# Three pairs of hidden blocks by seven half products in the last batch's first FFN product, and another order of the sums behind it

## The chip, the core and the metric

The kernel runs on one core of a Trainium2 chip. The time is the device time of one execution in microseconds (us), and the median of several executions is compared. A core has these engines: TensorE (PE, matrix products from SBUF into PSUM; loading the stationary operand is listed apart as PEld), VectorE (DVE), ScalarE (ACT), GpSimd (POOL) and SyncE (SP, which here issues output DMAs). Each works through its own instructions in the order in which the program wrote them, and waits on semaphores for the others. PSUM, where products accumulate, has eight banks of 512 fp32 columns.

## The reference

Attention with a band of local keys and 32 global tokens, then a feed-forward network (FFN) on all tokens. Here the second part matters:

```
x = attn_out.transpose(0, 2, 1, 3).reshape(8 * 544, 512)    # 8 batches, 32 global + 512 local rows each
h = x @ w_in                                                # 512 -> 2048
g = h * (1.0 / (1.0 + np.exp(-1.702 * h)))                  # "gelu" below
out = (g @ w_out).astype(np.float32)                        # 2048 -> 512
```

## The kernel before

The program is written in one fixed order, without a scheduler: an engine meets its instructions in the order in which the code names them. The local rows of batch `i` are one tile of 512 tokens, `xL[i]`, with features on the partitions. The first FFN product makes the 2048 hidden features as 16 **blocks** of 128 features by 512 tokens; the gelu of block `fc` goes to `gTs[i][:, fc]`. Two neighbouring blocks, `2g` and `2g+1`, are **pair** `g`.

A **direct step**, `h_step(i, fc)` (L663), takes a PSUM bank, runs four matmuls of 512 columns (`h_mm`, L636) and has ACT write the gelu (`h_act`, L659). Four banks (`pbank`) go round among these steps and other uses.

A pair can also be made with seven **half products** in place of the eight that two blocks of two token halves need (a Strassen-like scheme; a half product is two matmuls of 256 columns). That is class `HPair` (L698), for one pair or two at once: its PSUM tiles are `x` and `y` (of two banks each, from `spair`; one bank of each is used for a single pair), its sums of weights (`wh`) and of inputs (`xs`) are ready beforehand. Below, one use of it is called a triple of stages, or short a **triple**, whose operations are:

- `mm(3, 4)`: products 3 and 4 into the two halves of `x`; `m3`: ACT copies the half with 3 to an SBUF tile `zz`; `z` (L728): DVE adds the half with 4 to it;
- `mm(1, 6)`: products 1 and 6 into the two halves of `y`; `zm` (L731): DVE adds the half with 1 to `zz` as its other half;
- `mm(5, 2)`: accumulated on both halves of `x`; `sub` (L734): DVE takes `x` from `zz`; `inner`: ACT writes the gelu of `x`, which is two of the pair's four quarters;
- `mm(7)`: accumulated on the first half of `y`; `add` (L737): DVE adds `y` to `zz`; `outer`: ACT writes the gelu of `zz`, the other two quarters.

The second FFN product uses seven products as well, in class `Pair` (L796, matmuls in L821). Its operands are halves of `gTs[i]` and four arrays of sums and differences, which DVE makes in `g_sums(i, lo, hi, which)` (L785; L791 for array 2, L794 for arrays 0, 1 and 3) for the pairs `lo` to `hi - 1`, once their gelus are there. Product 3 reads the even blocks' first half of the tokens directly from `gTs`, product 4 the odd blocks' second half; 1, 6, 5 and 7 read arrays 0, 1, 2 and 3 (5 and 2 both read array 2).

`h_some(i)` (L1207) is the first FFN product of the batches 3 to 7. For 3 to 6 it has work of the next batches between (names `c` and `a2`), makes the pairs 1 and 2 in one triple and the rest directly, and returns early. For the last batch, 7, `c` and `a2` are `None`: it makes pair 1 in one triple, pair 4 in a second and the other twelve blocks directly. The sums of the gelus stand between its steps.

Behind it comes the tail (L1324 to L1378): the 256 global rows' first product (batch "B", 16 direct steps of four matmuls of 256 columns, `xG`) with the last batch's second product between its steps (`todo`, L1330), then the global rows' second product and the last stores. The tail's banks for `Pair` (`psX`) are the ones that `HPair` used. SP's queue holds the output stores; POOL only has two of the last ones here.

Of the kernel before, what the change touches and what calls it, by code (L numbers as in the profile page):

```python
# [20 lines left out]
def kernel(  # L21
# [53 lines left out]
    def load(b, us=(0, 1), kq=True):  # L75
        if b not in loaded:
            loaded[b] = (ld.tile([128, 2, 16 * D], BF16, name="rk"),
                         ld.tile([128, 2, 16 * D], BF16, name="rq"))
        if kq:
            s = slice(us[0], us[-1] + 1)  # L80
            nc.gpsimd.dma_start(out=loaded[b][1][:, s], in_=qf[b][:, s])
            nc.gpsimd.dma_start(out=loaded[b][0][:, s], in_=kf[b][:, s])
# [157 lines left out]
    def transpose_g(lo, hi, names="qk"):  # L240
        for name, dst, s in (("q", qgT, rqg), ("k", kgT, rkg)):
            if name not in names:
                continue
            nc.vector.transpose(dst[:, lo:hi, :32], s[:, lo:hi].bitcast(F32))
# [35 lines left out]
    def pbank(name):  # L280
        return psP.tile([128, 512], F32, name=name, tag="p")
# [349 lines left out]
    def width(i):  # L631
        return TB if i < B else B * Sg
# [3 lines left out]
    def h_mm(i, fc, hp, kcs):  # L636
        for kc in kcs:
            nc.tensor.matmul(hp[:, : width(i)], lhsT=w_in_c[:, fc // 4, kc, fc % 4 // 2, :, fc % 2],  # L638
                             rhs=(xL[i] if i < B else xG)[:, kc, :],
                             start=(kc == 0), stop=(kc == NKC - 1))  # L640
# [18 lines left out]
    def h_act(i, fc, hp):  # L659
        n = width(i)  # L660
        gelu(gTs[i][:, fc, :n], hp[:, :n])

    def h_step(i, fc):  # L663
        if fc == 0:
            gTs[i] = (moe.tile([128, FC, TB], BF16, name="gT") if i < B else
                      early.bitcast(BF16).rearrange("p a b -> p (a b)").rearrange("p (f t) -> p f t", f=FC))
        hp = pbank("hp")
        h_mm(i, fc, hp, range(NKC))
        h_act(i, fc, hp)
# [100 lines left out]
    def parts_of(i):  # L770
        n = width(i)
        t = gTs[i].rearrange("p (g e) t -> p g e t", e=2)
        return [t[:, :, e, h * n // 2 : h * n // 2 + n // 2] for h in range(2) for e in range(2)]

    def g_sums(i, lo, hi, which=(0, 1, 2, 3)):
        n = width(i)
        if i not in sums:
            if i < B:
                sums[i] = [moe.tile([128, FC // 2, w * HT], BF16, name="gs%d" % k)
                           for k, w in enumerate((1, 1, 2, 1))]  # L780
            else:
                room = [ld.tile([128, 2, 16 * D], BF16, name=x).rearrange("p a b -> p (a b)")
                        for x in ("rk", "rq", "rk")]
                sums[i] = [x.rearrange("p (g t) -> p g t", g=FC // 2)
                           for x in (room[0][:, :1024], room[0][:, 1024:], room[1], room[2][:, :1024])]  # L785
        a11, a12, a21, a22 = parts_of(i)
        t = gTs[i].rearrange("p (g e) t -> p g e t", e=2)
        g = slice(lo, hi)
        for k in which:
            if k == 2:  # L790
                nc.vector.tensor_tensor(sums[i][2][:, g, :n], t[:, g, 0, :n], t[:, g, 1, :n], ALU.add)  # L791
            else:
                x, y, op = {0: (a11, a22, ALU.add), 1: (a21, a11, ALU.subtract), 3: (a12, a22, ALU.subtract)}[k]
                nc.vector.tensor_tensor(sums[i][k][:, g, : n // 2], x[:, g], y[:, g], op)  # L794
# [75 lines left out]
    a, c = Quad(0), Quad(1)  # L870
# [94 lines left out]
    a, c = nq[1]  # L965
# [71 lines left out]
    a, c = nq[2]  # L1037
# [30 lines left out]
    def quads_of(n):  # L1068
        if n < B and n not in nq:
            nq[n] = (Wide(2 * n), Wide(2 * n + 1))  # L1070
        return nq.get(n, (None, None))
# [135 lines left out]
    def h_some(i):  # L1207
        c = nq[i + 1][1] if i + 1 < B else None
        a2 = quads_of(i + 2)[0] if i + 2 < B else None
        pool = nc.gpsimd.tensor_copy  # L1210
        gTs[i] = moe.tile([128, FC, TB], BF16, name="gT")
        hps = [pbank("hp"), pbank("hp")]
        for fc in range(2):
            h_mm(i, fc, hps[fc], range(NKC))
        gs = (1, 2) if c else (1,)
        fcs = iter([fc for fc in range(2, 8) if fc // 2 not in gs])
        p = HPair(i, *gs)
        p.mm(3, 4)
        p.m3()
        for fc in range(2):  # L1220
            h_act(i, fc, hps[fc])
        if c:
            if i + 3 < B:
                load(i + 3)
            c.kcopy(pool)
            c.qcopy(pool)
            c.ext((3,), pool)
        if a2:
            a2.Tk(False)
        p.z()  # L1230
        p.mm(1, 6)
        p.zm()
        if a2:
            a2.Tq(False)
            transpose_g(2 * i + 4, 2 * i + 6)
        h_step(i, next(fcs))
        if c:
            c.ext((0,), on_act)
        h_step(i, next(fcs))
        p.mm(5, 2)  # L1240
        p.sub()
        p.inner()
        p.mm(7)
        p.add()
        if not c:
            h_step(i, next(fcs))
            p.outer()
            h_step(i, next(fcs))
        else:
            g_sums(i, 0, 1)  # L1250
            h_step(i, 8)
            p.outer()
            g_sums(i, 1, 4)
            h_step(i, 9)
            c.ext((1,), on_act)
            h_step(i, 10)
            c.ext((2,), on_act)
            h_step(i, 11)
            h_step(i, 12)
            h_step(i, 13)  # L1260
            g_sums(i, 4, 7, (0, 1, 3))
            h_step(i, 14)
            h_step(i, 15)
            return
        p = HPair(i, 4)
        p.mm(3, 4)
        p.m3()
        g_sums(i, 0, 2, (0, 1))
        p.z()
        p.mm(1, 6)  # L1270
        p.zm()
        g_sums(i, 0, 2, (2,))
        h_step(i, 10)
        h_step(i, 11)
        p.mm(5, 2)
        p.sub()
        p.inner()
        p.mm(7)
        p.add()
        g_sums(i, 0, 2, (3,))  # L1280
        h_step(i, 12)
        p.outer()
        for k in range(3):
            for lo in (2, 4):
                g_sums(i, lo, lo + 2, (k,))
        h_step(i, 13)
        h_step(i, 14)
        h_step(i, 15)
        g_sums(i, 6, 8, (0, 1, 2))
        g_sums(i, 2, 4, (3,))  # L1290
        g_sums(i, 4, 6, (3,))
        g_sums(i, 6, 8, (3,))

    for i in range(1, B):
        if i > 2:
            h_some(i)
        elif i > 1:
            for fc in range(FC):
                h_step(i, fc)
                if i == 2 and fc == 0:  # L1300
                    weight_sums(1, 2)
                if i + 1 < B:
                    c = nq[i + 1][1]
                    if fc == 1:
                        c.Tk()
                        c.Tq()
                        c.ext((3,))
                    if fc in (3, 5, 7):
                        c.ext(((3, 5, 7).index(fc),), on_act)
                    if fc == 9 and i + 2 < B:  # L1310
                        a2 = quads_of(i + 2)[0]
                        a2.T()
                        transpose_g(2 * i + 4, 2 * i + 6)
                        a2.ext()
                if fc in (4, 8, 12):
                    g_sums(i, fc // 2 - 2, fc // 2)
                if fc == 13:
                    g_sums(i, 6, 7)
        if i == 1:
            phase_o1()  # L1320
        elif i + 1 < B:
            phase_o(i)
# [4 lines left out]
    def pair_banks(k):  # L1327
        return [psX.tile([128, 512], F32, name="x", tag="x%d" % (2 * (k % 2) + j)) for j in range(2)]

    todo = [(tt, k) for tt in range(2) for k in (3, 4, 1, 6, 5, 2, 7)]  # L1330
    for st in range(FC):
        h_step(B, st)
        if st < len(todo):
            tt, k = todo[st]
            if k == 3:
                p = Pair(B - 1, tt, pair_banks(tt))
# [19 lines left out]
    p = Pair(B, 0, (x0, x1, y0, y1))  # L1356
# [53 lines left out]
```

## Time and profile before

| | |
|---|---|
| median of three runs | 284.22 us (284.15, 284.22, 285.25) |
| the profiled execution | 284.39 us |
| its span, from first to last instruction | 282.7 us |
| last batch's first product on PE (starts in the timeline) | 240.21 to 253.62 us |
| busy from 240.20 to 254.06 us: PE, DVE, ACT, POOL | 13.86, 9.47, 10.79, 0.00 us |

A line of the page or of an answer names the line of the code, the engine, the operation, and the program's tiles as output<-input with their shapes; "xN" is the number of instructions in a group. In a line of the timeline, the first number is the start in us from the span's start, the second the time from there to the end of the group; in brackets stands the idle time ahead of it and what ended it. The chain of work that ended last goes back from the last instruction to what released it, step by step. The starts of matmuls are good marks; their ends are modelled, so that groups overlap a little in the list. An elementwise instruction on DVE or ACT can start a little (some 0.1 us) before the one ahead of it on its engine is listed as ended, where it doesn't need its result. The names in the lines: `s` is the tile of `HPair`'s `x` and `y`, `ob` the one of its `zz`, `hp` a direct step's bank, `gs` the arrays of sums, `px`, `py` and, in the tail, `x` the banks of the second product.

### The profile page before, as it was taken

To read this page: it belongs to the slowest core of one execution; us is meant where nothing else is said; L and a number is where in the kernel's file an instruction comes from. 1 tells how busy PE (TensorE), PEld (TensorE's weight loads), DVE (VectorE), ACT (ScalarE), POOL (GpSimd) and SP (SyncE) were. 2 spreads that over 40 slices of the span, in tenths; PEclk is the share of its full clock that TensorE was granted. 3 is DMA by queue.
4 is the path that set the end of the run, shared out by engine and by line. 5 is a ranking of instruction groups with operands and counts; after the bars stand their busy time and mean duration, and the time that the engine had idled before them with its cause. 6 is when DMAs were issued, how large, how long until landed. Compare 5 with 4: busy or idle time off the path is not lost.

```text
span 282.7 us, 9018 instructions
## 1 busy us (share of the span) xinstructions
PE 277.0 (98%) x3787; PEld 185.5 (66%) x3787; DVE 227.6 (81%) x486; ACT 186.9 (66%) x319; POOL 112.3 (40%) x161
## 2 busy tenths in 40 slices
PE   8999999999999999999999999999999999999994
PEld 7554445544554488756886488757876589558884
DVE  7687368996689898989998899899997898586452
ACT  4847657577778785489756994689648961873331
POOL 8984550856936004970099206940080000000001
PEclk9999999999999999999999999999999999999999
DMA  7999996999999804994089807930023003300223
GB/s 207 155 191 205 204 174 84 146 218 157 165 172 175 151 2 58 93 156 90 12 108 131 148 5 91 86 70 2 20 62 74 2 2 77 74 2 1 58 54 113
DMA packets 59352, 28.24 MB, mean 100 GB/s; under 512 B 47472, under 2 KB 49776, under 8 KB 59312
## 3 DMA queue, kind: packets, MB, share of 16 engines
q0 software_dynamic: 51760, 17.83, 57.1%
q1 hardware_dynamic: 7120, 9.18, 11.8%
q8 instruction: 29, 0.48, 0.7%
q10 hardware_dynamic: 432, 0.66, 0.7%
q14 instruction: 11, 0.09, 0.1%
HBM read 36.31 MB, written 8.91 MB: 160 GB/s over the span
## 4 chain that ended last, share of the span: by engine, by line
PE 93%; DMA 2%; DVE 2%; ACT 1%; SPq 0%; issue 0%; DVEq 0%
PE hp L638 32%; PE px L821 13%; PE op L752 10%; PE py L821 9%; PE x L821 6%; PE s L560 6%; PE s L720 5%; PE ov L586 5%; PE s L638 3%; DMA early<-in_q_l_dram 2%; DVE xL L471 1%; PE og L597 1%; PE s L357 1%; ACT e L388 1%; PE s L340 1%; PE ov L438 1%
## 5 line engine op out<-in xcount | busy, mean ns | idle before, releaser
L638 PE MATMUL hp<-xL,w_in_sb 128*128 128x512 bf16 x400 | 90.1, 379 | 0.2 <-DVE xL L471 0.2
L638 PEld LDWEIGHTS <-w_in_sb 128*128 128x128 bf16 x496 | 48.2, 98 | 48.1 <-issue 0.4
L643 ACT ACTIVATE gT<-hp 128x512 bf16<-128x512 f32 x100 | 57.1, 602 | 13.4 <-PE hp L638 13.0
L571 ACT ACTIVATE e<-s 128x1016 bf16<-128x1016 f32 (+1 forms) x56 | 53.3, 1003 | 17.9 <-PE s L560 17.9
L98 POOL DMA_DIRECT2D v<-in_v_l_dram x40 | 31.0, 779 | 61.3 <-PE og L597 52.6
L821 PEld LDWEIGHTS <-gs 128*128 128x128 bf16 x480 | 46.3, 98 | 6.4
L794 DVE TENSOR_TENSOR gs<-gT 128x256 bf16<-128x256 bf16 (+2 forms) x75 | 28.2, 406 | 4.7 <-ACT gT L643 4.7
L576 POOL TENSOR_TENSOR e<-e,mask 128x1760 bf16<-128x1760 bf16 (+1 forms) x7 | 23.1, 3305 | 19.1 <-ACT e L571 19.0
L821 PE MATMUL py<-wsum,gs 128*128 128x256 bf16 x240 | 30.3, 273 | 0.0
L752 PE MATMUL op<-w_out_sb,gT 128*128 128x512 bf16 x128 | 29.5, 380 | 0.0
L854 POOL DMA_DIRECT2D out_dram<-ob x2 | 1.2, 597 | 65.1 <-ACT ob L113 64.9
L576 DVE TENSOR_TENSOR e<-e,mask 128x1712 bf16<-128x1712 bf16 (+1 forms) x21 | 22.1, 1053 | 3.3 <-ACT e L571 3.1
L512 DVE STREAM_TRANSPOSE kT<-rk 128x512 f32<-128x512 f32 x14 | 14.7, 1047 | 11.0 <-DMA rk<-in_k_l_dram 11.0
L752 PEld LDWEIGHTS <-gT 128*128 128x128 bf16 x128 | 11.8, 98 | 14.0
L821 PEld LDWEIGHTS <-gT 128*128 128x128 bf16 x192 | 18.0, 98 | 2.9
L821 PE MATMUL px<-w_out_sb,gT 128*128 128x256 bf16 x160 | 19.2, 273 | 0.0
L821 PE MATMUL px<-w_out_sb,gs 128*128 128x256 bf16 x160 | 19.1, 273 | 0.0
L471 DVE TENSOR_TENSOR xL<-ov,rs 128x512 bf16<-128x512 f32 x27 | 17.9, 686 | 0.7 <-PE ov L438 0.3
L113 ACT ACTIVATE ob<-px 128x512 f32<-128x512 f32 x10 | 6.0, 599 | 18.7 <-DVE zz L843 18.7
L560 PEld LDWEIGHTS <-kT 32*128 32x128 bf16 x672 | 12.5, 93 | 6.8 <-issue 5.3
L643 ACT ACTIVATE gT<-s 128x1024 bf16<-128x1024 f32 (+1 forms) x10 | 9.3, 938 | 11.1 <-DVE ob L734 6.6
L791 DVE TENSOR_TENSOR gs<-gT 128x1024 bf16<-128x1024 bf16 (+3 forms) x21 | 15.9, 761 | 0.0
(182 smaller groups left out, 458.8 us busy)
## 6 DMA issues: line engine op xcount, KB each, us to landing
out_dram<-ob SPq DMA_DIRECT2D x128, 64.0 KB, 2.5
rq<-in_q_l_dram POOLq DMA_DIRECT2D x5, 512.0 KB, 5.2
rk<-in_k_l_dram POOLq DMA_DIRECT2D x5, 512.0 KB, 7.9
v<-in_v_l_dram POOLq DMA_DIRECT2D x24, 96.0 KB, 4.0
w_in_sb<-in_moe_w_in_dram POOLq DMA_DIRECT2D x8, 256.0 KB, 7.8
w_out_sb<-in_moe_w_out_dram POOLq DMA_DIRECT2D x4, 512.0 KB, 10.1
rk<-in_k_l_dram POOLq DMA_DIRECT2D x5, 256.0 KB, 7.4
rq<-in_q_l_dram POOLq DMA_DIRECT2D x5, 256.0 KB, 6.9
```

What stands on the lines that cost most here:

```text
L98: nc.gpsimd.dma_start(out=vt[0:n, hs, c, :D], in_=vs[FIRST[c] : FIRST[c] + n, hs])
L471: nc.vector.tensor_mul(self.x[:, 2 * self.u + h, :], self.st[1 + h], self.st["rs"])
L512: nc.vector.transpose(flat[:, 0:Sl].rearrange("p (r t) -> p t r", t=16), loaded[self.b][0][:, self.u].bitcast(F32))
L560: nc.tensor.matmul(bank(self.ps, j)[:, at : at + n], lhsT=self.k[p, KEYS[c] : KEYS[c] + 128, e], rhs=qs[p, :, :, e], start=(e == 0), stop= ...
L571: nc.scalar.activation(self.E[rnd][:, 2 * i : 2 * i + 2, :n], self.ps[i][:, :, :n], AF.Exp, scale=scale)
L576: eng.tensor_mul(e, e, mask[:, rnd : rnd + 1, :n].to_broadcast([128, 4, n]))
L638: nc.tensor.matmul(hp[:, : width(i)], lhsT=w_in_c[:, fc // 4, kc, fc % 4 // 2, :, fc % 2], rhs=(xL[i] if i < B else xG)[:, kc, :], start=( ...
L643: nc.scalar.activation(out_, in_, AF.Gelu_apprx_sigmoid)
L752: nc.tensor.matmul(op, lhsT=gTs[i][:, fc, tci * 128 : tci * 128 + 128], rhs=w_out_sb[:, fc, :], start=(first and fc == 4 * f4), stop=(fc = ...
L791: nc.vector.tensor_tensor(sums[i][2][:, g, :n], t[:, g, 0, :n], t[:, g, 1, :n], ALU.add)
L794: nc.vector.tensor_tensor(sums[i][k][:, g, : n // 2], x[:, g], y[:, g], op)
L821: nc.tensor.matmul(out_, lhsT=lv[:, g, tt * 128 : tt * 128 + 128], rhs=rv[:, g, :], start=(g == 0 and k in ((1, 3, 4, 6) if self.apart els ...
```

## The change

Only `h_some` is changed, and only for the last batch. The first triple makes the pairs 1 and 2 at once, as in the batches before. The direct steps are then 0, 1, 6, 7 and 10 to 15. The sums of pair 0 are made between the first triple's `zm` and `sub`. Steps 11 and 12 come before the second triple (pair 4), and only step 13 between its `mm(1, 6)` and its `mm(5, 2)`, where two steps were. The sums of the pairs 1 to 3 stand in two parts: arrays 0 and 1 between the second triple's `zm` and `sub`, arrays 2 and 3 behind its `add`. The sums of the pairs 4 to 7 come last, in the order of the arrays.

```diff
-        gs = (1, 2) if c else (1,)
+        gs = (1, 2)
         fcs = iter([fc for fc in range(2, 8) if fc // 2 not in gs])
...
         p.mm(1, 6)
         p.zm()
+        if not c:
+            g_sums(i, 0, 1)
...
         p.inner()
         p.mm(7)
         p.add()
-        if not c:
-            h_step(i, next(fcs))
-            p.outer()
-            h_step(i, next(fcs))
-        else:
+        if c:
             g_sums(i, 0, 1)
             h_step(i, 8)
             p.outer()
...
             return
+        h_step(i, 10)
+        p.outer()
+        h_step(i, 11)
+        h_step(i, 12)
         p = HPair(i, 4)
         p.mm(3, 4)
         p.m3()
-        g_sums(i, 0, 2, (0, 1))
         p.z()
         p.mm(1, 6)
         p.zm()
-        g_sums(i, 0, 2, (2,))
-        h_step(i, 10)
-        h_step(i, 11)
+        g_sums(i, 1, 4, (0, 1))
+        h_step(i, 13)
         p.mm(5, 2)
         p.sub()
         p.inner()
         p.mm(7)
         p.add()
-        g_sums(i, 0, 2, (3,))
-        h_step(i, 12)
+        g_sums(i, 1, 4, (2, 3))
+        h_step(i, 14)
         p.outer()
-        for k in range(3):
-            for lo in (2, 4):
-                g_sums(i, lo, lo + 2, (k,))
-        h_step(i, 13)
-        h_step(i, 14)
         h_step(i, 15)
-        g_sums(i, 6, 8, (0, 1, 2))
-        g_sums(i, 2, 4, (3,))
-        g_sums(i, 4, 6, (3,))
-        g_sums(i, 6, 8, (3,))
+        for k in range(4):
+            g_sums(i, 4, 8, (k,))
```

## The prediction

> **What bounds the kernel now.** I read the page's first two parts first (who is busy, at which clock), then the chain of work that ended last, in order of time, from the last batch on.
>
> ```profile
> PE 277.0 (98%) x3787; PEld 185.5 (66%) x3787; DVE 227.6 (81%) x486; ACT 186.9 (66%) x319; POOL 112.3 (40%) x161
> PEclk9999999999999999999999999999999999999999
> PE 93%; DMA 2%; DVE 2%; ACT 1%; SPq 0%; issue 0%; DVEq 0%
> ```
>
> TensorE (PE) is the bound: 93% of the chain is its own work, at the full granted clock. The chain in order of time, around the change:
>
> ```profile
> 240.37 1.73 PE hp L638 x8
> 242.10 0.87 PE s L720 x8
> ...
> 249.68 0.66 PE s L720 x6
> 250.33 3.89 PE hp L638 x20
> 254.22 0.87 PE x L821 x8
> ...
> 273.00 6.13 PE x L821 x56
> 279.15 0.42 DVE ob L1378
> ```
>
> From 240.37 to 279.13 us each piece begins where the last one ended. So in the last batch PE never waits, whatever PE saves there comes off the end, and whatever PE is made to wait there is added to it. Times below are starts in the timeline (some 0.16 us before the chain's), where the stage begins at 240.21 and the last batch's direct blocks end at 253.62.
>
> **PE work removed and added.** Before, one pair of blocks (2 and 3) and one more (8 and 9) are made with seven half products, the other twelve blocks directly; after, blocks 4 and 5 too go by half products. The chain gives eight full matmuls (one direct pair) 1.73 us, so 216 ns each, and eight half matmuls 0.87 us, so 109 ns each. A direct pair is 8 x 216 = 1.73 us; seven products of two matmuls are 14 x 109 = 1.53 us. PE does **0.20 us less**. Nothing else leaves PE, and no DMA, table load or GpSimd instruction is added or moved; the 128 output stores stay where they were on SP's queue.
>
> A rule of the Trainium skill speaks against this term: "TensorE: Matmul & The Clock Gate", section "Back-to-back issue gap", gives about 131 ns per 512-column matmul and 81 ns per 128-column one in a stream of loads and matmuls. On the straight line between them, an estimate from that page, 256 columns take 98 ns, and the pair would cost 14 x 98 - 8 x 131 = 0.32 us more instead of 0.20 less. The rows above (216 and 109 ns) don't agree with it, and they decide.
>
> **The first triple, two pairs at once.** Batch 6 runs the same two-pair triple in the profile, from its stage start at 210.39; adding 29.82 us puts its rows on the last batch. These are the ACT (ScalarE) rows and then the DVE (VectorE) rows there:
>
> ```profile
> 217.91 1.02 ACT L643 ACTIVATE gT<-s 128x1024 bf16<-128x1024 f32 x1 [1.28 <-DVE ob L734]
> 218.83 0.59 ACT L643 ACTIVATE gT<-hp 128x512 bf16<-128x512 f32 x1
> 219.31 1.06 ACT L643 ACTIVATE gT<-ob 128x1024 bf16<-128x1024 f32 x1
> 220.26 0.60 ACT L643 ACTIVATE gT<-hp 128x512 bf16<-128x512 f32 x1
> ```
>
> ```profile
> 216.66 1.22 DVE L734 TENSOR_TENSOR ob<-ob,s 128x1024 f32<-128x1024 f32 x1 [0.67 <-PE s L720]
> 217.98 1.22 DVE L737 TENSOR_TENSOR ob<-ob,s 128x1024 f32<-128x1024 f32 x1
> ```
>
> The reader sees a chain: sub (L734) 0.2 us after its last product, inner gelu only when sub has ended, then one direct gelu, outer gelu 0.11 us after add (L737), then a direct gelu 0.95 us later. On the last batch: sub 246.48, inner 247.73, gelu of block 10 at 248.65, outer 249.13, gelu of block 11 at 250.08. The wider m3 (0.58 us for 0.37) ends at 243.59, z and zm at 0.69 us each end at 245.11, the four sums of pair 0 end at 246.06 (batch 6's take 1.03 us): all before the products that need them (products 5 and 2 arrive at 245.41 and 7 at 246.28), and before sub. They cost **nothing**, hidden under steps 6 and 7; the tightest slack is 0.4 us (sums against sub).
>
> **The second triple, one pair: the first wait.** Unstalled, PE runs steps 10, 11 and 12 from 246.72, products 3, 4, 1, 6 of blocks 8 and 9 from 249.31 (their banks are free: inner ends at 248.75, add at 249.02), step 13 from 250.19, and wants product 5 at **251.05**. But m3 of this triple now stands on ACT behind the gelus of 11 and 12. Gelus follow each other every 0.48 us, so 12 starts at 250.56 and m3 at 251.04. What comes after m3 is in before's own second triple (ACT row, then DVE rows; L728 is z, L731 zm):
>
> ```profile
> 247.86 0.40 ACT L113 ACTIVATE ob<-s 128x256 f32<-128x256 f32 x1
> ```
>
> ```profile
> 248.29 0.42 DVE L728 TENSOR_TENSOR ob<-ob,s 128x256 f32<-128x256 f32 x1
> 248.81 0.42 DVE L731 TENSOR_TENSOR ob<-ob,s 128x256 f32<-128x256 f32 x1
> ```
>
> z 0.43 us after m3's start, zm 0.52 us after z, 0.42 us each. There products 5 and 2 started at 249.51, two steps after product 6, and found all done; after the change one step is left between, and ACT is later. So z runs 251.47 to 251.89 and zm 251.99 to 252.42. Products 5 and 2 overwrite the halves that m3 and z read, and 7 the half that zm reads. From DVE's end to PE's start I take 0.05 us, from the one place where PE waited for DVE (the first xL product of batch 1 ends at 52.81):
>
> ```profile
> 52.12 1.29 DVE L471 TENSOR_TENSOR xL<-s,rs 128x512 bf16<-128x512 f32 x2
> 52.86 0.59 PE L638 MATMUL hp<-xL,w_in_sb 128*128 128x512 bf16 x2 [0.16 <-DVE xL L471]
> ```
>
> Product 5 starts at 251.94 (0.89 us late), 7 at 252.47 for 252.38 (0.09 more): **+0.98 us**. If product 5 could start when m3 alone is done, 7 still waits for zm, with the same sum. Behind product 5 in PE's queue stand steps 14 and 15 and the whole tail; nobody else is held up. Bounds: 0.8 us (all latencies nil) to 1.2 us (0.1 us more at each of two crossings).
>
> **The second wait.** On DVE the sums 0 and 1 of pairs 1 to 3 (1.03 us, as batch 6's two of 768 columns) now stand between zm and sub: sub starts at 253.29, not at 252.6, where its products are there. Then inner at 254.01 (0.60 us), gelu 14 at 254.51, outer at 254.98 (after add, which ends at 254.77) until **255.61**, gelu 15 until 256.09. PE ends step 15 at 254.42 (253.62 - 0.20 + 0.98 = 254.40), does the first step of the last product's global rows to 254.86, and starts product 3 of the output stage (L821): its first four matmuls take 0.44 us, and its fifth loads block 8, whose half the outer gelu writes. It is wanted at 255.30, and can start at 255.72: **+0.42 us**. Bounds: 0 (if sub were taken before the sums) to 0.86 (if the wait stands before the first of the eight). Before, this product's start at 254.06 was ahead of the end of block 15's gelu (253.82 + 0.60 = 254.42), so matmuls wait for the blocks that they read and not for the whole tile; that is why I take 0.42.
>
> **The last sums.** Pairs 4 to 7 are summed after gelu 15: from 256.13, at 0.69 us for 1024 columns three times (L791 shows 684 ns for 1024) and 1.22 for 2048: the four end at 256.8, 257.4, 258.6 and 259.2. Products 1, 6, 5 and 7 want them at 257.9, 259.2, 260.5 and 263. The z of the output stage, queued on DVE behind them, ends at 259.5, and product 5 at 260.5 is the first to need its bank. Slack 1.0 us: **nothing**; beyond that it would cost its excess.
>
> **The sum.** -0.20 + 0.98 + 0.42 = **+1.20 us**. The profiled execution took 284.39 us, 282.7 of them its span; it would be 285.6. The runs shown have a median of 284.22 (284.15 to 285.25), 0.17 below the profiled one, so **285.4 us**, 0.42% more. A difference under 0.5% (1.42 us) is what I count as no change that a measurement of this kernel can tell.
>
> **Rivals.**
> - A. Neither wait: the pairs only save their 0.20 us, **284.0**. For it: PE had no wait at all in this stage before. Against it: the row that puts m3 behind two more gelus. Chance 0.07.
> - B. Only the first wait: sub comes early enough that the outer gelu is done at 255.3, or the wait falls on a later matmul, **285.0**. Against it: the order of DVE's instructions. Chance 0.15.
> - C. Slower: the wait for the outer gelu stands before the first matmul of product 3 instead of the fifth, so that those four (0.44 us) are late too: +1.64, **285.9**, 0.58% more. It decides from 0.22 us on over the sum. For it: waits are set by the program's bookkeeping of parts of a tile, and the outer gelu writes two separate quarters in one instruction. Against it: the 254.06 row. Chance 0.17.
> - D. Half products cost their weight loads: the loads take 98 ns in the rows against 109 ns of spacing, and with full matmuls at a shorter spacing the added pair would lose what it saves and more: with a loss of 0.32 us, +1.72, **285.9**. The page's rule above is this case; the 216 ns rows speak against it. Chance 0.02.
>
> The forecast, both waits as sized, has 0.59 and a range of its own of 285.1 to 285.7. A is within 0.5% as well: no case is faster by more, since PE saves 0.20 us at most. Slower by over 0.5%: C, D and the upper edge of the forecast (0.1 of it, and the spread of the runs), 0.28; faster 0.01; same 0.71. The range reaches from between A and B to beyond C and D with the upper bounds of both waits (1.2 and 0.86 give +1.86): **284.4 to 286.3**.
>
> **What would show it.** Right: the chain no longer runs through PE alone at 251 us but goes over ACT's m3 and DVE's z and zm (L728, L731), with some 0.9 us without matmuls before product 5 of the second triple; the first triple's rows lie at batch 6's times plus 29.82; sub of the second triple starts right behind two sums; a gap of 0.4 us stands inside the first L821 group of eight; and from there to the end everything is shifted alike. Wrong: no gap at 251 (A), an unbroken first L821 group (B) or one that starts late as a whole (C), spacings other than 109 ns in the added triple (D), or a shift that still grows after 256 us, which would mean that the last sums or the output stage's z are late, which I cost at nothing.

## The result, and the profile after

The changed kernel took 286.25 us (median of 7 executions, 285.66 to 286.92) against 284.89 us of the kernel before (7 executions, 284.15 to 285.33) measured beside it: ratio **1.0059, with a 95% interval of 1.0046 to 1.0072** (the medians alone give 1.0048). By the ratio that is slower by a little more than the 0.5% that the prediction took as its bound, where "the same" had the largest chance; the interval reaches below the bound. The profiled execution took 285.66 us, 283.7 of them its span.

The page of the kernel after, engines and chain:

```profile
PE 275.0 (97%) x3770; PEld 185.2 (65%) x3793; DVE 229.0 (81%) x482; ACT 186.8 (66%) x317; POOL 112.3 (40%) x161
PEclk9999999999999999999999999999999999999999
PE 91%; DVE 3%; ACT 3%; DMA 2%; issue 1%; SPq 0%; DVEq 0%; ACTq 0%
```

PE's share of the chain fell from 93 to 91%, ACT's rose from 1 to 3% and DVE's from 2 to 3%. (PE's busy time is no measure here: some matmul records are missing, 23 of them beside 3793 weight loads.) The chain that ended last, in order of time, in the last batch's stage:

```profile
248.30 1.03 PE hp L638 x4
249.33 0.45 PE s L720 x4
...
249.94 1.09 ACT gT L643 x2
251.03 0.28 ACT ob L113
...
251.33 0.43 DVE ob L728
...
251.86 0.42 DVE ob L731
252.28 0.06 DVE gs L794
252.34 0.33 issue
252.66 0.55 DVE gs L794
253.22 0.61 DVE ob L734
...
253.85 1.61 ACT gT L643 x3
255.46 0.05 issue
255.50 0.61 PE x L821 x4
```

Before, PE stood in every line from 240.37 to 279.13. Now the chain leaves PE at 249.8 and comes back at 255.5: two gelus, m3 (L113), z (L728), zm (L731), two sums (L794), sub (L734), then inner, gelu 14 and outer on ACT, and only then the tail's product 3. The same on PE, in the timeline of PE's matmuls after:

```profile
240.06 1.89 PE L638 MATMUL hp<-xL,w_in_sb 128*128 128x512 bf16 x7
...
250.04 1.03 PE L638 MATMUL hp<-xL,w_in_sb 128*128 128x512 bf16 x4
251.81 0.60 PE L720 MATMUL s<-xL,early 128*128 128x256 bf16 x4 [0.74 <-DVE ob L728]
252.33 0.38 PE L720 MATMUL s<-rs,early 128*128 128x256 bf16 x2
252.55 1.89 PE L638 MATMUL hp<-xL,w_in_sb 128*128 128x512 bf16 x8
254.28 0.60 PE L638 MATMUL hp<-xG,w_in_sb 128*128 128x256 bf16 x4
254.71 0.60 PE L821 MATMUL x<-w_out_sb,gT 128*128 128x256 bf16 x4
255.50 0.61 PE L821 MATMUL x<-w_out_sb,gT 128*128 128x256 bf16 x4 [0.19 <-ACT gT L643]
255.95 0.60 PE L638 MATMUL hp<-xG,w_in_sb 128*128 128x256 bf16 x4
```

Before, the same product 3 and the step behind it:

```profile
254.06 1.04 PE L821 MATMUL x<-w_out_sb,gT 128*128 128x256 bf16 x8
254.93 0.60 PE L638 MATMUL hp<-xG,w_in_sb 128*128 128x256 bf16 x4
```

After, the four matmuls of step 13 start at 250.04 and take 0.87 us (four spacings of 216 ns), so product 5 was due at 250.91 and starts at 251.81; the eight matmuls of the tail's product 3 are split after the fourth, which would have been followed at 255.15 and is followed at 255.50.

For all kernels below I read one number, the **stage time**: from the first `hp` group of the last batch to the second `xG` group, both on PE. Before it is 240.21 to 254.93, 14.72 us; after 240.06 to 255.95, 15.89 us: **1.17 us more**, where the prediction has 1.20. After that the tail's pieces run at the same distances in both: 27.75 us to the end of the span.

### The profile page after: what moved, and what is told of

It reads as the page before. It is cut to its first block, busy times and chain, and to the rows that moved or that the text cites. A ratio compares the mean times of both kernels' runs of the same rounds, so it can differ in the third digit from the quotient of the medians.

```text
span 283.7 us, 9001 instructions
## 1 busy us (share of the span) xinstructions
PE 275.0 (97%) x3770; PEld 185.2 (65%) x3793; DVE 229.0 (81%) x482; ACT 186.8 (66%) x317; POOL 112.3 (40%) x161
## 4 chain that ended last, share of the span: by engine, by line
PE 91%; DVE 3%; ACT 3%; DMA 2%; issue 1%; SPq 0%; DVEq 0%; ACTq 0%
PE hp L638 30%; PE px L821 13%; PE op L752 10%; PE py L821 9%; PE x L821 6%; PE s L560 6%; PE s L720 6%; PE ov L586 5%; PE s L638 2%; DMA early<-in_q_l_dram 2%; ACT gT L643 1%; DVE xL L471 1%; PE og L597 1%; PE s L357 1%; ACT e L388 1%
## 5 line engine op out<-in xcount | busy, mean ns | idle before, releaser
L638 PE MATMUL hp<-xL,w_in_sb 128*128 128x512 bf16 x377 | 86.9, 379 | 1.0 <-DVE xL L471 0.2
L638 PEld LDWEIGHTS <-w_in_sb 128*128 128x128 bf16 x488 | 47.4, 98 | 47.1 <-issue 0.4
L643 ACT ACTIVATE gT<-hp 128x512 bf16<-128x512 f32 x98 | 56.1, 603 | 12.7 <-PE hp L638 12.3
L821 PEld LDWEIGHTS <-gs 128*128 128x128 bf16 x480 | 46.2, 98 | 6.5
L794 DVE TENSOR_TENSOR gs<-gT 128x256 bf16<-128x256 bf16 (+3 forms) x72 | 28.0, 417 | 3.7 <-ACT gT L643 3.6
L821 PE MATMUL py<-wsum,gs 128*128 128x256 bf16 x240 | 30.3, 273 | 0.0
L752 PE MATMUL op<-w_out_sb,gT 128*128 128x512 bf16 x122 | 28.8, 380 | 0.5 <-issue 0.3
L821 PEld LDWEIGHTS <-gT 128*128 128x128 bf16 x192 | 17.8, 98 | 3.4 <-ACT gT L643 0.5
L821 PE MATMUL px<-w_out_sb,gT 128*128 128x256 bf16 x160 | 19.2, 273 | 0.0
L821 PE MATMUL px<-w_out_sb,gs 128*128 128x256 bf16 x160 | 19.1, 273 | 0.0
L113 ACT ACTIVATE ob<-px 128x512 f32<-128x512 f32 x10 | 6.0, 599 | 18.7 <-DVE zz L843 18.7
L791 DVE TENSOR_TENSOR gs<-gT 128x512 bf16<-128x512 bf16 (+3 forms) x20 | 15.8, 791 | 0.0
```

The costliest lines, as they stand in the source:

```text
L643: nc.scalar.activation(out_, in_, AF.Gelu_apprx_sigmoid)
L752: nc.tensor.matmul(op, lhsT=gTs[i][:, fc, tci * 128 : tci * 128 + 128], rhs=w_out_sb[:, fc, :], start=(first and fc == 4 * f4), stop=(fc = ...
L821: nc.tensor.matmul(out_, lhsT=lv[:, g, tt * 128 : tt * 128 + 128], rhs=rv[:, g, :], start=(g == 0 and k in ((1, 3, 4, 6) if self.apart els ...
```

## The experiments

The theory: PE waits twice, because m3 stands behind two gelus on ACT whose chain is wider now, and because two sums stand ahead of sub on DVE; nothing else. The rivals are in the expectations. Ratios are against the kernel before on the same chip, beside the same runs.

**The changed kernel again**, without an edit, since 1.17 us is 0.41% and the ratio 0.59%.

> The changed kernel as it is, once more. In its profile the last batch's stage and the start of the tail cost 1.17 us more than before's (the third group of the tail's first steps starts 16.04 instead of 14.87 us behind the stage's start or so, read at the second global step), while the medians are 1.36 us and the ratio of all runs 0.59% (1.7 us) apart. Theory (two waits of PE and nothing else): the profile repeats the two gaps, and the ratio comes out nearer to 1.0041. Rival (something outside this stage costs 0.2 to 0.5 us more): ratio 1.005 to 1.007 again, with a difference of spans or of the time outside the span that the stage does not show.

Measured: ratio 1.0038 (1.0025 to 1.0051), stage time 239.88 to 255.77, 15.89 us. (The two times that the expectation names for the stage are 0.15 us too long; by the marks above they are 14.72 and 15.89.) The stage repeats to the hundredth, the ratio doesn't.

**m3 ahead of the gelus 11 and 12 on ACT.**

```diff
-        h_step(i, 11)
-        h_step(i, 12)
+        hps = [pbank("hp"), pbank("hp")]
+        for fc in (11, 12):
+            h_mm(i, fc, hps[fc - 11], range(NKC))
         p = HPair(i, 4)
         p.mm(3, 4)
         p.m3()
+        for fc in (11, 12):
+            h_act(i, fc, hps[fc - 11])
```

> The changed kernel with the second triple's m3 ahead of the gelus of blocks 11 and 12 on ACT; PE's and DVE's order is kept. Theory (m3's place on ACT sets the first wait): m3 about 1 us earlier, product 5 and 7 of the second triple wait 0.0 to 0.1 us, the second wait stays near 0.4 us (the two sums still stand ahead of sub on DVE); 0.2 to 0.3 us over before, ratio 1.001. Rival (one direct step is too little between products 6 and 5, whatever ACT does, since z and zm take 0.95 us on DVE): the first wait stays at 0.5 us or more, ratio 1.003 or more.

Measured: ratio 1.0008 (0.9994 to 1.0022), stage time 14.91 us, 0.19 over before. m3 starts at 249.89, straight behind outer. PE's rows:

```profile
250.85 0.60 PE L720 MATMUL s<-xL,early 128*128 128x256 bf16 x4
251.52 1.89 PE L638 MATMUL hp<-xL,w_in_sb 128*128 128x512 bf16 x8
...
254.48 0.61 PE L821 MATMUL x<-w_out_sb,gT 128*128 128x256 bf16 x4 [0.20 <-ACT gT L643]
```

The stage began at 240.01, and product 5 starts 10.84 us later, with nothing ahead of it; in the changed kernel it was 11.75. Step 14 follows product 5 by 0.67 us, six matmuls at 109 ns. So the first wait is gone and the second stays: one step between products 6 and 5 is enough once ACT is in time. The rival falls.

**The sums behind add.**

```diff
         p.zm()
-        g_sums(i, 1, 4, (0, 1))
         h_step(i, 13)
...
         p.add()
-        g_sums(i, 1, 4, (2, 3))
+        g_sums(i, 1, 4)
```

> The changed kernel with the arrays 0 and 1 of pairs 1 to 3 summed behind the second triple's add, with arrays 2 and 3, and not between zm and sub. Theory: the first wait stays (0.9 us ahead of product 5, 0.1 ahead of 7), sub starts about 0.7 us earlier, outer ends before the tail's product 3 wants block 8, so the second wait is gone; the later sums stay within their slack; 0.78 us over before, ratio 1.0027. Rival (the second gap is not made by sub's place, or the sums are what is late next): a gap of 0.3 us or more stays in the first L821 group or moves to product 1, 5 or 2 of the tail, ratio 1.004.

Measured: ratio 1.0032 (1.0018 to 1.0046), stage time 240.35 to 255.87, 15.52 us, 0.80 over before. DVE from zm on, and then the chain behind the first wait:

```profile
252.14 0.42 DVE L731 TENSOR_TENSOR ob<-ob,s 128x256 f32<-128x256 f32 x1
252.73 0.69 DVE L734 TENSOR_TENSOR ob<-ob,s 128x512 f32<-128x512 f32 x1 [0.16 <-PE s L720]
```

```profile
252.09 0.91 PE s L720 x6
253.00 2.16 PE hp L638 x12
255.16 0.87 PE x L821 x8
```

Sub follows zm by 0.59 us (1.27 in the changed kernel, 251.86 to 253.13), and from product 5 on the chain is PE's again; the first L821 group is whole. The first wait is as in the changed kernel. The later sums moved nothing.

**Both edits.**

> Both edits: m3 ahead of the two gelus, and the sums behind add. Theory: no gap on PE from the stage's start to the end; 0.20 us less than before, ratio 0.9993. Rival (something outside the two waits costs time): ratio above 1.001 with an unbroken chain on PE in this stage, the difference then lying elsewhere in the span or outside it.

Measured: ratio 0.9992 (0.9978 to 1.0006), stage time 240.15 to 254.69, 14.54 us, **0.18 less than before**. The chain in this stage is PE alone (but for two pieces of 0.05 us "issue" ahead of these lines):

```profile
248.39 1.03 PE hp L638 x4
249.41 0.87 PE s L720 x8
250.29 0.86 PE hp L638 x4
251.15 0.67 PE s L720 x6
251.82 2.16 PE hp L638 x12
253.98 0.87 PE x L821 x8
```

So the third pair saves what its matmuls save, when nothing waits; a ratio can't tell 0.2 us from nothing.

**The order alone**: the changed kernel's order, with pair 1 alone in the first triple and blocks 4 to 7 as direct steps (6 and 7 stand around `outer`, 10 to 12 behind them).

> The changed kernel's order with the old work: the first triple makes pair 1 alone, blocks 4 to 7 are direct steps; one step between products 6 and 5 of the second triple, and the sums in the new places. Theory (the first wait comes of ACT's backlog behind the two-pair triple, whose sub, inner, add and outer are twice as wide): with one pair ACT keeps up, m3 starts 0.5 us after the gelu of block 12 and about 9.98 us after the stage's start, products 5 and 7 wait 0.0 to 0.1 us; the sums ahead of sub still hold up the outer gelu and product 3 of the tail waits 0.3 us; 0.35 us over before, ratio 1.0012. Rival (the order alone makes the first wait): product 5 waits 0.5 us or more, ratio 1.003 or more.

Measured: ratio 1.0015 (1.0006 to 1.0023), stage time 240.32 to 255.34, 15.02 us, 0.30 over before. Its ACT rows:

```profile
249.82 0.60 ACT L643 ACTIVATE gT<-hp 128x512 bf16<-128x512 f32 x1 [0.27 <-PE hp L638]
250.31 0.38 ACT L113 ACTIVATE ob<-s 128x256 f32<-128x256 f32 x1
```

The gelu of block 12 waits for PE, so ACT has no backlog; m3 comes 0.49 us behind it, 9.99 us after the stage's start (10.83 in the changed kernel, 240.06 to 250.89), and product 5 finds z done. The second wait is there (0.30 us). The first wait needs the two-pair triple and the new order together; the second comes with the order of the sums alone. (The two-pair triple in before's order was not run.)

**Step 14 into the first gap.** `h_step(i, 14)` is moved from behind the sums to behind step 13.

> The changed kernel with step 14 moved ahead of products 5, 2 and 7 of the second triple, so that PE has 0.87 us of work where it waited 0.89 us. Theory (the end is set by the chain m3, z, zm, two sums, sub, inner and add, outer on ACT and DVE, which doesn't move): the first gap shrinks to 0.1 us in all, and the gap in the first L821 group grows from 0.35 to about 1.2 us; the total stays 1.1 to 1.2 us over before, ratio 1.004. Rival (the first gap is a cost of its own, and PE's work in it is won): 0.3 to 0.4 us over before, ratio 1.001.

Measured: ratio 1.0045 (1.0029 to 1.0061), stage time 240.16 to 255.87, 15.71 us, 0.99 over before. The end of its chain, and PE's rows there:

```profile
254.01 0.70 DVE ob L737
...
254.74 0.64 ACT gT L643
...
255.42 0.61 PE x L821 x4
```

```profile
253.51 0.60 PE L638 MATMUL hp<-xG,w_in_sb 128*128 128x256 bf16 x4
254.76 1.27 PE L821 MATMUL x<-w_out_sb,gT 128*128 128x256 bf16 x8 [0.65 <-DVE ob L737]
```

PE works through the gap at 251 and could start the tail's product 3 at 253.95. But it starts at 254.76, no earlier than in the changed kernel (254.71): it waits for add (L737), which ends at 254.71, 0.81 us in all. In the changed kernel add was done at 254.61, 0.10 us before product 3 was due. And its fifth matmul comes at 255.42 for 255.20, behind outer, another 0.22 us. Of the 0.87 us of work moved into the gap, 0.18 were won, because outer no longer stands behind gelu 14; I had said 0.0 to 0.1. The rest came back as a wait of 1.03 us, most of it ahead of the first matmul of the eight and not of the fifth, where I had looked for it. The chain on ACT and DVE set the end.

**A third measurement of the changed kernel, and the kernel before against itself.**

> The changed kernel once more, since the first measurement gave a ratio of 1.0059 (1.0046 to 1.0072) and the second 1.0038 (1.0025 to 1.0051), with the same 1.17 us in the stage in both profiles. Theory (1.17 us is all): ratio 1.0035 to 1.0047. Rival (0.5 us more lie outside the stage): 1.0055 or more.

> The kernel before, measured against itself, to see how far a ratio of this kind lies from 1 when nothing is changed. Theory (the scatter of the runs explains the distance between 1.0038 and 1.0059): a ratio within 0.001 to 0.0015 of 1. Rival: exactly 1 within 0.0003, so that the distance would be a real difference between the two measurements.

Measured: 1.0063 (1.0050 to 1.0076), stage time 15.90 us; and 1.0001 (0.9992 to 1.0009). Both went to the rival: the kernel before agrees with itself within 0.0001, and the changed one is again 0.6% slower. So something beside the stage does cost time, and not always. An execution's time is its span and what lies outside it, and the latter tells them apart:

| kernel (executions) | mean span, us | mean outside the span, us | over 1.87 us outside |
|---|---|---|---|
| before, beside all the experiments (90) | 282.78 | 1.72 (1.66 to 1.84) | 0 |
| order alone (12) | 283.17 | 1.71 (1.66 to 1.75) | 0 |
| changed, first, second and third (25) | 283.90 | 2.07 (1.67 to 2.99) | 16 |
| m3 first, sums behind add, both (36) | 283.00 | 1.91 (1.66 to 2.89) | 14 |
| step 14 into the gap (6) | 283.92 | 1.87 (1.66 to 2.36) | 2 |

The spans differ by 1.12 us, as the stage says. Outside them the kernels with the two-pair triple lose another 0.15 to 0.35 us on average. What they have in common is 12 more instructions of PE (six loads, six matmuls), and the last three runs tested that.

**PE's program longer and shorter.** The number of warm-up matmuls at the kernel's start is changed, which fill a wait for the first loads and whose results aren't used: 27 for 21 in the kernel before, 15 for 21 in the version with both edits and in the changed kernel.

```diff
-    fill(21, psP.tile([128, 512], F32, name="w", tag="p"), True)
+    fill(27, psP.tile([128, 512], F32, name="w", tag="p"), True)
```

> The kernel before with 27 instead of 21 warm-up matmuls at its start (they fill a wait for the first loads and compute nothing that is used), which gives PE's program as many instructions as the changed kernel has (12 rows more). What is tested: the time of an execution that lies outside its span. It was 1.66 to 1.84 us in all 69 executions of before and 1.66 to 1.75 in the 12 with the order alone, but over 2.2 us in 7 of 25 of the changed kernel, and in 6 of 42 of the four kernels derived from it that keep its two-pair triple. Theory (the length of PE's program makes it): some of these executions lie over 2.2 us outside the span, with a mean of 1.85 to 2.1. Rival (something else in the two-pair kernels, or chance): all between 1.66 and 1.85 us. The span is 282.8 us by both.

> Both edits (m3 ahead of the two gelus, sums behind add), with 15 instead of 21 warm-up matmuls, so that PE's program is as long as before's. Theory (program length): 1.66 to 1.85 us outside the span in every execution; span 282.5 us, so 0.2 us less than before, ratio 0.9993. Rival: executions over 2.2 us outside the span as without this edit (2 of 12 there, mean 1.92).

> The changed kernel with 15 instead of 21 warm-up matmuls, so that PE's program is as long as before's. Theory (program length): 1.66 to 1.85 us outside the span in every execution, span 283.8 to 283.9, ratio 1.0039 to 1.0043. Rival: as the changed kernel, a mean of 1.9 to 2.2 us outside the span, ratio 1.0045 to 1.006.

(The count "6 of 42" in the first of them is 5.) Measured:

| kernel (executions) | ratio | mean span, us | mean outside, us | over 1.87 us |
|---|---|---|---|---|
| before, longer (11) | 1.0021 (1.0009 to 1.0033) | 283.24 | 1.88 (1.66 to 2.61) | 4 |
| both edits, shorter (11) | 0.9991 (0.9982 to 1.0000) | 282.50 | 1.72 (1.67 to 1.87) | 0 |
| changed, shorter (5) | 1.0040 (1.0027 to 1.0052) | 283.92 | 1.70 (1.68 to 1.73) | 0 |

The theory holds: with 12 more instructions of PE the kernel before gets the long executions, and with 12 fewer the changed kernel and the version with both edits lose them. (The longer one's span is also 0.46 us above before's on average, which I had not expected; its stage time is 14.73 us, so that lies elsewhere.) In its profiled execution, with a span of 283.5 us, nearly all of the excess over 282.7 is one gap of PE at 19.8 us, amid eight matmuls that run without one in the kernel before:

```profile
19.41 0.39 PE L638 MATMUL s<-xL,w_in_sb 128*128 128x512 bf16 x1
20.50 1.67 PE L638 MATMUL s<-xL,w_in_sb 128*128 128x512 bf16 x7 [0.71 <-issue]
```

The profile shows nothing that PE waits for there; the cause is open.

Without the 12 instructions the changed kernel's ratio is what its stage gives, 1.17 us or 0.41%. Over all kernels with 3793 weight loads, 36 of 78 executions have over 1.87 us outside the span, and 14 of them over the 2.2 us that the expectations name; over all with 3787, none of 118. (1.87 is the largest value of those 118; the line was drawn there afterwards.)

## Why the prediction failed in its verdict and held in its working

- **The work** (0.20 us less): right. With both edits the stage is 0.18 us shorter. The spacing of 109 and 216 ns holds in the added triple (its first sixteen `s` matmuls, from 242.04, take 1.75 us in the chain of the version with both edits), and case D is out.
- **The first triple** at batch 6's times plus 29.82 us: right. The stage began 0.15 us earlier in the profiled execution; with that taken off, inner was forecast at 247.58, the gelu of block 10 at 248.50, outer at 248.98 and m3 at 250.89. ACT's rows of the kernel after:

```profile
247.59 1.02 ACT L643 ACTIVATE gT<-s 128x1024 bf16<-128x1024 f32 x1 [1.53 <-DVE ob L734]
248.51 0.59 ACT L643 ACTIVATE gT<-hp 128x512 bf16<-128x512 f32 x1
248.99 1.06 ACT L643 ACTIVATE gT<-ob 128x1024 bf16<-128x1024 f32 x1
249.94 1.09 ACT L643 ACTIVATE gT<-hp 128x512 bf16<-128x512 f32 x2
250.89 0.41 ACT L113 ACTIVATE ob<-s 128x256 f32<-128x256 f32 x1
```

- **The first wait** (0.98 us): right. Product 5 came 0.90 us late and 7 another 0.08 (252.33, 0.52 us behind product 5, where four matmuls take 0.44). Taking m3 forward removes it. Product 5 accumulates on the half that m3 read, which was done at 251.30, and yet starts only after z, done at 251.75, which read the other half of the same bank. The Trainium skill, "PSUM — Partial Sum Buffer", section "PSUM bank collisions raise a hardware error", says that two engines have to be kept apart by bank and not by address. The program's wait in these rows goes by the bank; no run here shows what would happen without it.
- **The second wait** (0.42 us): right in place, before the fifth matmul, and a little large: 0.35 us (255.50 for 255.15). The forecast had 0.11 us from outer's end to the fifth matmul (255.61 to 255.72); it took 0.05. Moving the sums removes it. Cases A, B and C are out: C's 285.9 lies near the measured time for another reason.
- **The last sums at nothing**: right; the tail runs at before's distances, and 1.02 us of sums moved behind add cost nothing either.
- **The step that failed** is the sum, "-0.20 + 0.98 + 0.42 = **+1.20 us**", put whole on the time of an execution. It holds for the span (1.17 us) and has no term for what lies outside the span, which was taken over from before as 1.69 us (284.39 less 282.7). The change costs there too, by the six loads and six matmuls that make PE's program longer. In the seven executions of the first measurement 2.23 us lay outside the span on average, against 1.72 in the 90 of before: 0.51 us, or 0.18%. The term varies: 0.20 us in the second measurement, 0.50 in the third. So "the same" lost, and slower won by a cost that no case had; without the longer program it is 1.0040, as forecast. Which side of 0.5% a measurement fell on was partly luck: the three ratios are 1.0059, 1.0038 and 1.0063, and the mean of all 25 executions is 0.52% above that of the 90. Before's own executions scatter too: the seven beside the first measurement averaged 284.72 us, 0.22 above the 90.

What stays open: why a longer PE program costs time outside the span in some executions, whether it is the length or where some part of it comes to lie, at which length it begins, and whether it comes before the first or after the last instruction. The Trainium skill, "Runtime: NRT & Kernel Launch", section "Instruction fetch mechanics", says that an engine fetches its program in blocks of 16 KiB, mostly hidden. Within the span the page of the profile counts 29 instruction packets and 0.48 MB on that queue for the long and the short kernels alike. But the trace of the third measurement, whose profiled execution has 2.99 us outside its span, holds a 30th, behind the last instruction at 283.73 us. This is what its DMA view has from 283.8 to 290 us:

```profile
DMA packets 1, 0.02 MB, mean 3 GB/s; under 512 B 0, under 2 KB 0, under 8 KB 0
q8 instruction: 1, 0.02, 1.5%
```

The packet starts at 285.54 and ends at 287.00 us. The run with step 14 in the gap has one too, from 284.10 to 284.97, with only 1.73 us outside; the other six profiles with the longer program have none, though four of them have 1.92 to 2.00 us outside, and neither have the five with the shorter one. So the two lengths may differ by a block that is fetched around the program's end, but a wait for it is not shown: the packet of the third measurement ends later than its execution would (286.69 us) if that began with the first instruction.

## What to carry to other kernels

When one half product in eight is replaced by sums and copies on other engines, follow the whole chain that now stands between two products: here a saving of 0.18 us of PE's work came with 1.35 us of waiting, because an instruction that PE would need soon stood behind others that nobody needed yet. Order an in-order engine's queue by who waits first; filling PE's gap with later work instead lost 0.69 of the 0.87 us again to other waits. And where a difference of a few tenths of a us counts, split each time into its span and the rest before explaining it.

## What the runs showed of the hardware

Twelve more PE instructions in a program of 7574 weight loads and matmuls gave executions with 1.9 to 3.0 us outside the span, where 118 executions with the shorter programs had 1.66 to 1.87; it happened in 36 of 78. It was shown by lengthening the kernel before and shortening two others. The step from another engine to PE was short at the two waits of the changed kernel: 0.06 us from z's end (251.33 + 0.42) to product 5 at 251.81, and 0.05 (the chain's "issue") from outer's end at 255.46 to the fifth matmul.
